# One DMA for the short set's rising rows, an earlier second gate chunk, Z cleared one step sooner, and newly searched units

## The chip, the cores and the metric

The kernel runs on one core of a Trainium2 chip. The metric is device time in microseconds (us) of one execution. The engines are TensorE (PE in the profile, its weight loads PEld), VectorE (DVE), ScalarE (ACT), GpSimd (POOL) and SyncE (SP, which here only issues DMAs). An engine's name with a q behind it (SPq) is its instruction queue.

## The reference

A two-dimensional Fourier transform of each of 8 sequences, its real part, and a SwiGLU block on the result.

```
x: [8, 3008, 256] f32;  w_gate, w_val: [256, 1536];  w_out: [1536, 256]
X = fft(fft(x, axis=1), axis=2).real          -> 24064 tokens of 256
g = X @ w_gate;   silu = g / (1 + exp(-g));   val = X @ w_val
out = (silu * val) @ w_out
```

## The kernel before

**What is computed where.** The real part of the transform is even under turning both frequencies, so the kernel computes for half of the tokens an even part (Pt) and an odd part (Qt). A token and its mirror are then made of the same two products, with Pt and Qt combined by plus and by minus. The transform along the 256 features is folded into the gate and value weights: Wp is the weights times a cosine table (CD), Wq the weights times a sine table (SDt), and Wm is Wq with the factor that the mirrored token needs. The transform along the 3008 rows is done by adding rows in pairs ("folding"), which shortens it, and then multiplying with cosine and sine tables (Tab).

**Prologue (lines 254 to 649).** It is written out by hand, engine by engine. Batch 0 is loaded in two sets: a long one into XA (128 partitions) and a short one into XC0. Rows that count upward ("rising") come in one way, rows that count downward ("falling") in another. For the short set, `rise_c` (line 263) is called twice, each time for one block of rising rows, and `fall_c` (line 266) four times for the falling ones. All of these go out from SyncE's queue. Permuting matmuls (`place`, line 431) put the rows in order, VectorE, GpSimd and ScalarE fold them (`cross`, `half_fold`, `fold_d`, `ends`, `heads`), and TensorE multiplies with Tab (`half_folded`, `folded_c`, `row0`), which gives Pt and Qt of the first tiles (`first_puts`). ScalarE fills the tables; `opposite(1)` (line 543) fills the last one, the negated columns for the short set, and the activation on line 544 clears Z0, a buffer of zeros. From Z0 two DMAs on SyncE (line 546) clear unused rows of XC, and behind them on the same queue go the first rows of batch 1 (`load_c`, lines 155 to 164).

The weights come in three chunks of 512 columns, gate and value apart, by DMAs that GpSimd issues (`load_w`, line 387). Chunk 0 goes into buffers of its own, chunks 1 and 2 into the part of XA that held the rising rows of batch 0. Each chunk is multiplied with CD and SDt on TensorE (`first_w`, line 500, for chunk 0; `weight_op`, line 1432, for the others, with the matmuls on line 1442). In GpSimd's order the loads of chunks 1 and 2 stand together, behind two folds `fold_d(1, 0)` and `fold_d(1, 2)` (line 495), the sum EOb (line 555) and the two `heads` adds for CEc (lines 462 and 463).

**Main part (lines 923 to 1667).** 24 tiles of mostly 512 half-set tokens, 12 units of 128 hidden columns in each: 288 units. A unit multiplies Pt and Qt with Wp, Wq and Wm (line 972) into PSUM tiles g and v, and ScalarE, VectorE and GpSimd make from them the two hidden products hp (the token) and hm (the mirrored one). The products of one tile are multiplied with w_out during the next tile (line 1236), copied out of PSUM (line 1243) and stored. In between stand the folds of later batches (GpSimd, lines 178 to 202), their transforms (line 1394) and the loads.

One digit per unit in `KINDS` says how it is done. The lowest bit: the value is "seeded", that is ScalarE writes a row into PSUM ahead of the matmuls (line 1045) and copies the even value out (line 1107), in place of one VectorE operation (line 1109). The second bit: the gate is split on VectorE, which saves one of the unit's five matmuls. From 4 on: ScalarE copies the value out and GpSimd makes hp (line 1192), from 8 on also the mirrored value (line 1195). A `w` unit does everything by whole matmuls.

The order of all this is made by a planner in the kernel itself (class `Sched`, line 767). Every operation gets a due time, that is the sum of TensorE's planned work so far plus a shift by kind (`SHIFT`) plus a correction by tile and kind (`BIAS_ROWS`). The planner then walks through planned time engine by engine and takes, within a window, what can start first. It uses planned durations, `W_AT` for the times at which the weight chunks of 1 and 2 land, and the start times of the engines that are given to `S.run` on the last line. What it decides is each engine's order of instructions, which the chip follows as it stands.

Of the kernel before, what the change touches and what calls it, by code (L numbers as in the profile page):

```python
# [15 lines left out]
AF = mybir.ActivationFunctionType  # L16
# [3 lines left out]
def kernel(  # L20
# [8 lines left out]
    nc = tc.nc  # L29
    B, M, D = x.shape  # L30
    Dff = moe_w_gate.shape[1]
    P = 128
# [3 lines left out]
    R = M // 4  # L36
# [53 lines left out]
    zero = const.tile([P, 1], F32, name="zero")  # L90
# [6 lines left out]
    Z0 = const.tile([P, 2, 3, P], BF16, name="Z0")  # L97
# [27 lines left out]
    def rows_at(b, row, ap):  # L125
        return bass.AP(tensor=x.tensor, offset=(b * M + row) * D, ap=ap)
# [124 lines left out]
    XC3 = XC0.rearrange("p a q d -> p a (q d)")  # L251
    q = nc.sync
# [7 lines left out]
    def fall_a(a, eng):  # L260
        eng.dma_start(out=XA3[:, 4 + a, :], in_=down_set(0, a, JA, LA, NA))

    def rise_c(a, eng):
        eng.dma_start(out=XC3[:, a, :], in_=rows_at(0, 2 * (P + 1) - 1 + a * R, [[2 * D, 64], [2 * R * D, 2], [1, 2 * D]]))

    def fall_c(hi, a, eng):
        eng.dma_start(out=XC3[64 * hi:64 * hi + NCR, 2 + a, :], in_=down_set(0, 3 - 2 * hi - a, JC, LC, NC_))
# [3 lines left out]
    fall_a(2, q)  # L271
    fall_a(1, nc.scalar)
    fall_a(0, q)
    for a in range(2):
        rise_c(a, q)

    iota = dict(channel_multiplier=0, allow_small_or_imprecise_dtypes=True)
    pcol = tp.tile([P, 1], F32, name="pcol")
# [102 lines left out]
    def opposite(ch):  # L381
        nc.scalar.activation(Tab[:, ch, :, :, NCE:NOO - 1], Tab[:, ch, :, :, GH + 1:NCE], AF.Copy, scale=-1.0)
# [1 line left out]
    def weigh_ce():  # L384
        nc.scalar.activation(Tab[:, 1, 1, :, 0:NCE], Tab[:, 1, 1, :, 0:NCE], AF.Copy, scale=wC)

    def load_w(c, only=(0, 1)):
        for i, src in ((0, moe_w_gate), (1, moe_w_val)):
            if i not in only:
                continue  # L390
            w_ = src.rearrange("(no p) f -> p no f", p=P)[:, :, c * T:(c + 1) * T]
            nc.gpsimd.dma_start(out=Wraw[i][:, :, (c - 1) * T:c * T] if c else W0[i], in_=w_)
# [10 lines left out]
                        in_=rows_at(0, 0, [[2 * R * D, 2], [R * D, 2], [1, D]]))  # L403
# [56 lines left out]
    def heads(ev, od, CE):  # L460

        ptt(CE[:, :, 0, 0, -1:], ev, od, op=Alu.add)
        ptt(CE[:, :, 0, 1, -1:], ev, od, op=Alu.subtract)
# [12 lines left out]
    def set_cols(ps, tab, a):  # L476
        if a % 2:
            return (ps[:, 0:2 * GH + 2].rearrange("p (t n) -> p t n", t=2),
                    tab[:, 0:2 * NCE].rearrange("p (t n) -> p t n", t=2)[:, :, 0:GH + 1])
        return ps[:, 0:NCE], tab[:, 0:NCE]  # L480

    def half_folded(eo, a0, first):
        for q in range(2):
            for a in range(a0, a0 + 2):
                dst, rhs = set_cols(acc[eo][q], Tab[:, 0, q, eo], a)
                nc.tensor.matmul(dst, EOb[:, eo, a, q, :], rhs, start=first and a == a0, stop=False, skip_group_check=True)

    def folded_c(eo, a, first=False):
        for q in range(2):
            dst, rhs = set_cols(acc[eo][q], Tab[:, 1, q, eo], a)  # L490
            nc.tensor.matmul(dst, EB[:, eo, a, q, :], rhs, start=first and a == 0, stop=a == 1, skip_group_check=True)

    def fold_d(eo, a0):
        F = FA[:, a0:a0 + 2]
        ptt(EOA[eo][a0 // 2], F[:, :, :, P:0:-1], F[:, :, :, P:D], op=SUMS[eo])

    def half_cast(eo, a0):
        nc.scalar.copy(EOb[:, eo, a0:a0 + 2], EOA[eo][a0 // 2])
# [24 lines left out]
    for a in range(2):  # L523
        ends(Eh[:, a], XA, psA, a)
    row_signs()
    load_w(0, (0,))
    fold_d(0, 0)
    load_w(0, (1,))
    fold_d(1, 0)
    for a in range(2, 4):  # L530
# [9 lines left out]
    for a in range(2, 4):  # L540
        nc.scalar.copy(FA[:, a, :, P + 1:D], psA[a][:, :, P + 1:D])
    half_cast(0, 2)
    opposite(1)
    nc.scalar.activation(Z0.rearrange("p q k d -> p (q k d)"), zero.to_broadcast([P, 6 * P]), AF.Copy)
    for hi in range(2):
        q.dma_start(out=X3c[64 * hi + NCR:64 * hi + 64, :].rearrange("p (c d) -> p c d", d=D),
                    in_=zeros[64 * hi + NCR:64 * hi + 64].unsqueeze(1).to_broadcast([64 - NCR, 16, D]))
    loads_c1 = load_c(1, q)
    for load in loads_c1[:C1_EARLY]:
        load()  # L550
    fold_d(1, 2)
    hd = tp.tile([P, 2, 2, 1], F32, name="hd")
    ptt(hd, Eh[:, 0:2], Eh[:, 2:4], op=Alu.add)
# [16 lines left out]
    for a in range(2):  # L570
        folded_c(1, a, True)
    half_folded(1, 0, False)
    heads(Ec0[:, 0], Ec0[:, 1], CEc)
    load_w(1)
    load_w(2)
    for k in range(2):
        pts(BBc[:, :, 1, k, 0:1], Ec0[:, 1 - k], scalar1=(nsgn, sgn)[k], scalar2=1.0, op0=Alu.mult, op1=Alu.mult)
    nc.gpsimd.iota(kfO, pattern=[[4, GH]], base=1, **iota)
# [104 lines left out]
    def rows(r0, n, step):  # L683
# [31 lines left out]
        "PUT": -2.8,  # L715
    }
    BIAS_ROWS = (
# [24 lines left out]
    )  # L742
    BIAS = {(t, k): v for t, row in enumerate(BIAS_ROWS) for k, v in zip(SHIFT, row)}
    ES_BUFS = 2
# [7 lines left out]
    GRP = 4  # L752
    AHEAD = 1
    WM_ACT = ()
    W_AT = (1.4, 2.8, 4.4, 6.0)
    SIGN_AT = 8
    class Op:
        __slots__ = ("eng", "dur", "lat", "fn", "at", "n", "deps", "owners", "new", "ring", "slots", "start", "end", "users")
# [161 lines left out]
    def pool_us(n):  # L920
# [6 lines left out]
    ROW_PE = {ROW_1: 1, ROW_2: 2, ROW_3: 3}  # L927
    KINDS = (
        "wwwwwwwwwwww",
        "06ww20001033",  # L930
        "031303160011",
        "010112310133",
        "010210112013",
        "10010b003133",
        "001211031052",
        "003171700001",
        "331213005030",
        "010271031100",
        "34130b310300",
        "01b300700101",  # L940
        "21312101b200",
        "001371310011",
        "70520031b212",
        "10310b030310",
        "001430103130",
        "413370000411",
        "213b21011200",
        "103b11309610",
        "0030b13300b0",
        "616444563010",  # L950
        "143034169230",
        "706120713313",
    )

    def whole(u):
# [18 lines left out]
    S = Sched()  # L974
# [631 lines left out]
    for fc in (1, 2):  # L1606
        for gv in range(2):
            S.add("DMA", 0.01, lambda: None, w=[(("W",), (fc, gv))], lat=W_AT[2 * fc - 2 + gv])
    S.add("DMA", 0.01, lambda: None, w=[(("pq", 0), "Q")], lat=0.1)
# [54 lines left out]
    part_b(prev)  # L1664
    owork = OWork(prev[0], ((psG, "g"), (psV, "v"), (psO, "o")))
    owork.run(len(owork.steps))
    S.run({'DVE': 1.5, 'ACT': 1.0, 'POOL': 1.6, 'PE': 0.0, 'SP': 1.0})


# [28 lines left out]
```

## Time and profile before

| | us |
|---|---|
| median of 3 runs | 603.52 |
| the 3 runs | 602.71, 603.52, 603.52 |
| the profiled execution's own time | 602.03 |
| its span, first to last instruction | 600.3 |
| TensorE busy in the span | 589.2 |
| first matmul of the main part's units | 19.07 |

How to read it: "busy" counts the time in which at least one instruction of the engine runs. Matmuls overlap, so their printed durations add up to more than their busy time; the distance from one start to the next is what a matmul costs. In a timeline a row has its start, its duration, engine, line, operation, tiles written and read, shapes, a count, and in brackets the idle time of the engine before it with what ended it. "DMA to landing" is the time from the start of the issue to the landing of the last byte.

### The profile page before, as it was taken

What the parts mean: (1) busy time and instruction counts of PE and PEld (TensorE: products, weight loads), DVE (VectorE), ACT (ScalarE), POOL (GpSimd) and SP (SyncE); (2) the same over time, 40 slices, a digit from 0 to 9 for tenths busy, and PEclk for the clock granted to TensorE, in tenths of its full rate; (3) what the DMA queues carried; (4) which work ended last, traced back from release to release, by engine and by line L of the source; (5) the groups of instructions that cost most, each with busy time, mean ns of one, the idle gap of its engine ahead of it and who ended that gap; (6) DMA issues with size and microseconds to landing.
All of it is one profiled execution on the core that took longest, in us unless ns stands there. A gap on an engine that the chain in (4) does not pass through costs nothing.

```text
span 600.3 us, 12453 instructions
## 1 busy us (share of the span) xinstructions
PE 589.2 (98%) x3950; PEld 390.3 (65%) x4012; DVE 568.3 (95%) x1063; ACT 556.4 (93%) x1081; POOL 529.1 (88%) x487
## 2 busy tenths in 40 slices
PE   9899999999999999999999999999999999999997
PEld 6356666666666666666666666666666666666686
DVE  8689999999999999999999999999999999999993
ACT  8587999999999999899999999998999999999994
POOL 8689999999799999999999999998898567687772
PEclk9899999999999999999999999999999999999999
DMA  9766347244625424444146122056221212111122
GB/s 243 117 125 131 108 124 183 77 131 117 157 81 123 126 69 120 112 142 127 55 96 144 45 55 72 19 119 157 62 63 37 64 31 70 55 44 45 50 62 80
DMA packets 51098, 57.65 MB, mean 96 GB/s; under 512 B 7299, under 2 KB 38455, under 8 KB 51033
## 3 DMA queue, kind: packets, MB, share of 16 engines
q1 hardware_dynamic: 47449, 53.91, 33.9%
q0 software_dynamic: 3216, 2.36, 2.8%
q8 instruction: 31, 0.51, 0.4%
q10 hardware_dynamic: 368, 0.59, 0.4%
q14 instruction: 34, 0.28, 0.2%
HBM read 29.43 MB, written 24.65 MB: 90 GB/s over the span
## 4 chain that ended last, share of the span: by engine, by line
PE 90%; ACT 3%; DMA 3%; POOL 2%; issue 1%; DVE 1%; SPq 0%; ACTq 0%; POOLq 0%
PE o L1236 38%; PE g L972 24%; PE v L972 20%; PE o L1394 2%; PE g L1394 2%; DMA XA<-in_moe_w_gate_dram 1%; DMA XA<-in_x_dram 1%; DMA out_dram<-ev 1%; PE o L304 1%; ACT sv L1159 1%; PE o L1442 1%; PE v L1236 1%; POOL hm L1183 1%; ACT v L1045 1%; ACT sp L1084 1%
## 5 line engine op out<-in xcount | busy, mean ns | idle before, releaser
L1183 POOL TENSOR_TENSOR hm<-sv 128x1024 bf16<-128x1024 f32 (+2 forms) x137 | 254.9, 1862 | 42.9 <-ACT sv L1159 25.1
L1175 DVE SCALAR_TENSOR_TENSOR sv<-es,v 128x512 f32<-128x512 f32 (+2 forms) x262 | 173.7, 669 | 4.8 <-PE v L972 3.5
L1236 PE MATMUL o<-Wo,hm 128*128 128x256 bf16 (+1 forms) x1128 | 164.2, 273 | 0.5
L1236 PE MATMUL o<-Wo,hp 128*128 128x256 bf16 (+1 forms) x1104 | 160.5, 273 | 0.6
L1186 DVE TENSOR_TENSOR hp<-sp,v 128x512 bf16<-128x512 f32 (+2 forms) x232 | 153.1, 669 | 2.2 <-ACT sp L1084 1.0
L1236 PEld LDWEIGHTS <-hm 128*128 128x128 bf16 (+2 forms) x1140 | 111.8, 98 | 57.6 <-issue 1.0
L1236 PEld LDWEIGHTS <-hp 128*128 128x128 bf16 (+2 forms) x1140 | 111.9, 98 | 56.3 <-issue 0.5
L1159 ACT ACTIVATE sv<-g 128x512 f32<-128x512 f32 (+2 forms) x179 | 119.0, 675 | 3.3 <-PE g L972 2.0
L1084 ACT ACTIVATE sp<-g 128x512 f32<-128x512 f32 (+2 forms) x179 | 110.4, 626 | 4.7 <-PE g L972 1.9
L1045 ACT ACTIVATE v<-bc,w 128x512 f32<-128x512 bf16 (+2 forms) x146 | 105.2, 721 | 1.2 <-DVE hp L1186 0.7
L972 PE MATMUL v<-Pt,Wp 128*128 128x512 bf16 (+2 forms) x285 | 105.0, 375 | 0.8
L972 PE MATMUL g<-Pt,Wp 128*128 128x512 bf16 (+2 forms) x282 | 105.5, 375 | 0.1
L1109 DVE SCALAR_TENSOR_TENSOR es<-bc,w,v 128x512 f32<-128x512 bf16 (+2 forms) x128 | 93.3, 733 | 2.5 <-POOL sv L1195 0.4
L1107 ACT ACTIVATE es<-v 128x512 f32<-128x512 f32 (+2 forms) x146 | 90.7, 623 | 3.8 <-DVE sv L1175 1.6
L972 PE MATMUL g<-Qt,Wq 128*128 128x512 bf16 (+2 forms) x247 | 90.9, 375 | 0.3
L972 PEld LDWEIGHTS <-Wp 128*128 128x128 bf16 x576 | 56.3, 98 | 27.3 <-issue 1.0
L972 PE MATMUL g<-Qt,Wm 128*128 128x512 bf16 (+2 forms) x188 | 70.8, 377 | 0.2
L1088 DVE SCALAR_TENSOR_TENSOR sg<-bc,w,g 128x512 f32<-128x512 bf16 (+2 forms) x95 | 68.6, 723 | 1.1 <-PE g L972 1.1
L1159 ACT ACTIVATE sv<-sg 128x512 f32<-128x512 f32 (+2 forms) x95 | 66.6, 705 | 1.7 <-DVE sg L1152 1.6
L1152 DVE SCALAR_TENSOR_TENSOR sg<-sg,g 128x512 f32<-128x512 f32 (+2 forms) x95 | 62.9, 662 | 0.4
L1156 ACT ACTIVATE sp<-g 128x512 f32<-128x512 f32 (+2 forms) x95 | 58.9, 620 | 2.1 <-DVE sg L1152 1.7
L1243 ACT COPY ev<-o 128x512 f32<-128x512 f32 x89 | 55.3, 621 | 4.3 <-PE o L1236 3.5
(218 smaller groups left out, 767.3 us busy)
## 6 DMA issues: line engine op xcount, KB each, us to landing
out_dram<-ev SPq DMA_DIRECT2D x96, 128.0 KB
XA<-in_x_dram SPq DMA_DIRECT2D x30, 256.0 KB
XA<-in_x_dram SPq DMA_DIRECT2D x112, 64.0 KB
XC<-in_x_dram SPq DMA_DIRECT2D x28, 120.0 KB
XC<-in_x_dram SPq DMA_DIRECT2D x105, 32.0 KB
bc<-br SPq DMA_DIRECT2D x19, 128.0 KB
St<-Fc SPq DMA_DIRECT2D x12, 128.5 KB
out_dram<-ev SPq DMA_DIRECT2D x12, 120.0 KB
```

The lines of the kernel that those rows point to most:

```text
L972: nc.tensor.matmul(ps[:, :n], Wt[:, gv, fs], src[:, :n], start=start, stop=stop, skip_group_check=True)
L1045: nc.scalar.activation(T_[kv][:, :w], bc[t][:, :w], AF.Copy, scale=w0[:, 1, f:f + 1])
L1084: nc.scalar.activation(sp_to()[:, :w], T_[kg][:, :w], AF.Silu)
L1088: nc.vector.scalar_tensor_tensor(T_[keg][:, :w], bc[t][:, :w], w0[:, 0, f:f + 1], T_[kg][:, :w], op0=Alu.mult, op1=Alu.add)
L1107: nc.scalar.activation(T_[kes][:, :w], T_[kv][:, :w], AF.Copy, scale=2.0 if on_pool(u) > 1 else 1.0)
L1109: nc.vector.scalar_tensor_tensor(T_[kes][:, :w], bc[t][:, :w], w0[:, 1, f:f + 1], T_[kv][:, :w], op0=Alu.mult, op1=Alu.add)
L1152: nc.vector.scalar_tensor_tensor(T_[kgm][:, :w], T_[keg][:, :w], 2.0, T_[kg][:, :w], op0=Alu.mult, op1=Alu.subtract)
L1159: nc.scalar.activation(sv()[:, f % 2, w - 1::-1, 1], T_[kgm if by_dve else kg][:, :w], AF.Silu)
L1175: nc.vector.scalar_tensor_tensor(sv()[:, f % 2, w - 1::-1, 0], T_[kes][:, :w], 2.0, T_[kv][:, :w], op0=Alu.mult, op1=Alu.subtract)
L1183: nc.gpsimd.tensor_tensor(hts_(t)[1][:, f - 1:f + 1, :w], sv()[:, :, :w, 1], sv()[:, :, :w, 0], op=Alu.mult)
L1186: nc.vector.tensor_tensor(hts_(t)[0][:, f, :wp], T_[ksp][:, :wp], T_[kv][:, :wp], op=Alu.mult)
L1236: nc.tensor.matmul(st["ps"][:n, j, :], hts[t][minus][:, f, c:c + n], Wo[:, f, :], start=(f == 0), stop=(f == nF - 1))
```

## The change

Four edits.

- The two rising-row DMAs of the short set become one with one more dimension (`rises_c`), with the same bytes to the same places.
- `load_w(1)` is split: the gate's chunk 1 is issued between `fold_d(1, 0)` and `fold_d(1, 2)` on GpSimd, the value's chunk 1 behind the EOb sum and ahead of the two `heads` adds for CEc. Chunk 2 stays behind these.
- Z0 is cleared ahead of `opposite(1)` on ScalarE instead of behind it.
- `BIAS_ROWS` (24 rows of 17 numbers), 16 rows of `KINDS`, `W_AT` and the start times for the planner are new numbers.

```diff
-    def rise_c(a, eng):
-        eng.dma_start(out=XC3[:, a, :], in_=rows_at(0, 2 * (P + 1) - 1 + a * R, [[2 * D, 64], [2 * R * D, 2], [1, 2 * D]]))
+    def rises_c(eng):
+        eng.dma_start(out=XC3[:, 0:2, :], in_=rows_at(0, 2 * (P + 1) - 1, [[2 * D, 64], [2 * R * D, 2], [R * D, 2], [1, 2 * D]]))
...
-    for a in range(2):
-        rise_c(a, q)
+    rises_c(q)
...
-    def load_w(c, only=(0, 1)):
+    def load_w(c, only):
...
     half_cast(0, 2)
+    nc.scalar.activation(Z0.rearrange("p q k d -> p (q k d)"), zero.to_broadcast([P, 6 * P]), AF.Copy)
     opposite(1)
-    nc.scalar.activation(Z0.rearrange("p q k d -> p (q k d)"), zero.to_broadcast([P, 6 * P]), AF.Copy)
...
         load()
+    load_w(1, (0,))
     fold_d(1, 2)
...
     half_folded(1, 0, False)
+    load_w(1, (1,))
     heads(Ec0[:, 0], Ec0[:, 1], CEc)
-    load_w(1)
-    load_w(2)
+    load_w(2, (0, 1))
...
-        (-13.7, -7.2, -11.75, -3.45, 3.2, -1.3, -1.15, 2.75, 7.55, -6.6, -9.45, -2, 3.85, -10.15, 18.65, -1.6, -4.05),
+        (-29.4, 13.3, 4.3, -0.95, -17.9, -7.05, 2.4, -8.1, -12.35, -6.85, -2.05, -18.8, -5.5, 1.6, -25.1, -6.8, -1),
...
-    W_AT = (1.4, 2.8, 4.4, 6.0)
+    W_AT = (0.0, 2.0, 3.2, 4.6)
...
-        "06ww20001033",
+        "06ww20001013",
...
-        "010112310133",
-        "010210112013",
-        "10010b003133",
-        "001211031052",
-        "003171700001",
+        "000010312133",
+        "010210112012",
+        "10110b103133",
+        "001601031052",
+        "300171700001",
...
-        "010271031100",
+        "010271031001",
...
-        "21312101b200",
+        "21312101b300",
...
-        "70520031b212",
-        "10310b030310",
-        "001430103130",
-        "413370000411",
+        "32120011b212",
+        "10130b135030",
+        "000135003170",
+        "033170001011",
...
-        "103b11309610",
-        "0030b13300b0",
-        "616444563010",
+        "103b10319610",
+        "4030b13300b0",
+        "616404563200",
...
-        "706120713313",
+        "706150233313",
...
-    S.run({'DVE': 1.5, 'ACT': 1.0, 'POOL': 1.6, 'PE': 0.0, 'SP': 1.0})
+    S.run({'DVE': 1.6, 'ACT': 1.0, 'POOL': 1.4, 'PE': 0.0, 'SP': 2.0})
```

46 rows, old and new, of the table BIAS_ROWS are left out of this document.

## The prediction

> **What bounds the kernel now.** I read the page first: the span, the busy time of each engine, and the chain of waits.
>
> ```profile
> span 600.3 us, 12453 instructions
> PE 589.2 (98%) x3950; PEld 390.3 (65%) x4012; DVE 568.3 (95%) x1063; ACT 556.4 (93%) x1081; POOL 529.1 (88%) x487
> PE 90%; ACT 3%; DMA 3%; POOL 2%; issue 1%; DVE 1%; SPq 0%; ACTq 0%; POOLq 0%
> ```
>
> TensorE (PE) is the bound: busy 98% of the span and 90% of the chain. So only two things can move the time: TensorE's idle or slowed stretches, and the number of its matmuls. Next came busy time by window. Columns: window; then us and count for PE, PEld, DVE, ACT, POOL; granted clock; DMA share; GB/s.
>
> ```profile
> 20.25:23.66 3.41, 1.18 (x7) 0.48 (x5) 1.31 (x4) 1.03 (x2) 3.36 (x8) 1.00 1.25 169
> 23.66:27.07 3.41, 3.41 (x10) 1.21 (x8) 1.13 (x2) 1.63 (x3) 1.43 (x2) 0.50 0.75 151
> 44.00:550.00 506.00, 502.92 (x3370) 333.68 (x3427) 494.37 (x884) 482.21 (x927) 464.20 (x396) 1.00 0.36 94
> 200.00:300.00 100.00, 99.37 (x668) 65.91 (x679) 98.76 (x180) 96.09 (x185) 98.17 (x85) 1.00 0.35 101
> ```
>
> From 44 to 550 TensorE is idle 3.1 us in 506, at full clock: there is almost nothing to win there, and much to lose, since the other three engines are 92 to 98% busy too. The one large hole is at 20 to 27 us: 3.41 us with 1.18 busy, then 3.41 us at half the clock. The timeline of TensorE says what is late there:
>
> ```profile
> 19.07 0.57 PE L972 MATMUL g<-Pt,Wp 128*128 128x480 bf16 x2
> 20.54 0.37 PE L972 MATMUL v<-Pt,Wp 128*128 128x480 bf16 x1
> 20.74 0.37 PE L972 MATMUL v<-Qt,Wq 128*128 128x480 bf16 x1
> 23.34 0.73 PE L1442 MATMUL o<-XA,CD 128*128 128x512 bf16 x2 [2.23 <-DMA XA<-in_moe_w_gate_dram]
> 27.50 0.59 PE L1442 MATMUL o<-XA,CD 128*128 128x512 bf16 x2
> 28.37 0.37 PE L972 MATMUL g<-Pt,Wp 128*128 128x480 bf16 x1
> 29.38 0.38 PE L1442 MATMUL o<-XA,CD 128*128 128x512 bf16 x1
> 31.66 0.59 PE L1442 MATMUL o<-XA,CD 128*128 128x512 bf16 x2
> ```
>
> The rows of L1442 are where the four remaining weight chunks are multiplied: gate 1 at 23.34, value 1 at 27.50, gate 2 at 29.38, value 2 at 31.66. Starts of L972 are 0.20 apart, so the first L1442 could have begun at 20.94: 2.40 us are lost to the gate's DMA. The half clock loses half of 3.41, 1.71 more. Together 4.1 us.
>
> **Part by part: the second gate chunk.** GpSimd's (POOL) timeline shows when the four chunks are issued. Behind it stands, for each of the four in that order, how long it took from issue to landing, and last the same for the value chunk before these, from the list of DMA issues.
>
> ```profile
> 11.33 1.11 POOL L495 TENSOR_TENSOR Fc<-FA 128x512 f32<-128x512 f32 x1
> 12.97 1.09 POOL L495 TENSOR_TENSOR Fc<-FA 128x512 f32<-128x512 f32 x1 [0.53 <-ACT FA L541]
> 14.61 1.27 POOL L555 TENSOR_TENSOR EOb<-Fc 128x512 bf16<-128x512 f32 x1
> 16.53 0.20 POOL L462 TENSOR_TENSOR CEc<-Ec 128x2 bf16<-128x2 f32 x1 [0.66 <-DVE Ec L453]
> 17.01 0.73 POOL L392 DMA_DIRECT2D XA<-in_moe_w_gate_dram  x1
> 17.74 0.74 POOL L392 DMA_DIRECT2D XA<-in_moe_w_val_dram  x1
> 18.46 0.73 POOL L392 DMA_DIRECT2D XA<-in_moe_w_gate_dram  x1
> 19.17 0.74 POOL L392 DMA_DIRECT2D XA<-in_moe_w_val_dram  x1
> ```
>
> ```profile
> DMA to landing us min/median/max: 6.3/6.3/6.3
> DMA to landing us min/median/max: 9.4/9.4/9.4
> DMA to landing us min/median/max: 10.1/10.1/10.1
> DMA to landing us min/median/max: 11.9/11.9/11.9
> ...
> W<-in_moe_w_val_dram POOLq DMA_DIRECT2D x1, 256.0 KB, 4.7
> ```
>
> Now they land at 23.3, 27.1, 28.6 and 31.1: each just ahead of its matmul, the first one after it. Gate 1 moves between the two folds, to about 12.45, four and a half us earlier. Its buffer's last readers, the placing matmuls, are done by 10, so it doesn't wait there. By 4.7 to 6.3 it lands at 17.1 to 18.8, well ahead of 20.94. That wait goes, and with it the half clock: -4.1.
>
> GpSimd pays 0.73 for the issue, of which 0.53 lies in an idle gap. Behind the issue on its queue stand the fold, three small adds and the EOb sum. L495's second fold starts at some 13.25, the EOb sum ends near 16.15 instead of 15.88. TensorE takes EOb at 16.71 (row below), so 0.5 us still cover it; without that cover it would cost the 0.3. Value 1 is then issued at 16.2, ahead of the two heads that waited until 16.53 anyway; they end near 17.3, and their readers start at 17.6.
>
> **What is late next.** Value 1 is now the first chunk under the load of SyncE's (SP) x rows, so I give it gate 1's 6.3: 22.5. TensorE wants it at 20.94 + 0.87 (four L1442, from 27.50 to 28.37) + 8 x 0.20 = 23.4. No wait, 0.9 to spare. Gate 2 is issued at 17.2; as second chunk, 9.4 gives 26.6, and the distance of first to second landing (27.1 - 23.3 = 3.8) gives 26.3. I take 26.4. The planner now takes it to land 3.2 after the first unit, at 19.07 + 3.2 = 22.3, and puts it after only three L972 instead of five: 23.4 + 0.87 + 0.61 = 24.9. So TensorE waits again, for 1.5 us. Value 2 comes 1.4 after gate 2 (28.6 - 27.1), at 27.8; it is wanted at 26.4 + 0.87 + 9 x 0.20 = 29.1 against 31.66 now. Net gain 2.6. The bounds: 0 new wait (4.1 gained), or the wait brings the half clock back (1.71 more, 0.9 gained).
>
> The row behind this is the 4.7 against 6.3 to 11.9 for equal chunks: those issued from 17 on are slower. The Trainium skill, DMA: Bandwidth & Descriptors, section on why a DMA increments its semaphore by 16, says that a transfer is spread over as many engines as divide its slowest dimension, and that the hardware queues take the lowest-numbered ones. By that, the zero fills and x rows of four partitions each all sit on the same four engines, where every chunk has a share, and gate 2 stays late: 600.9 by the sum below. Without it the 4.7 comes back and the time is 599.4. No view here names an engine.
>
> **The prologue edits.**
>
> ```profile
> 2.72 1.28 SPq L264 DMA_DIRECT2D XC<-in_x_dram  x2
> 4.04 6.47 SPq L267 DMA_DIRECT2D XC<-in_x_dram  x4
> 14.31 0.42 DVE L449 TENSOR_TENSOR FC<-o,XC 128x256 f32<-128x256 f32 x1 [0.39 <-DMA XC<-in_x_dram]
> 14.04 0.84 ACT L544 ACTIVATE Z<-zero 128x768 bf16<-128x768 f32 x1
> 14.90 1.49 SPq L546 DMA_DIRECT2D XC<-Z  x2
> 15.71 0.33 PE L491 MATMUL v<-Tab,EOf 128*128 128x378 bf16 x1 [0.25 <-DVE EOf L458]
> 16.71 0.48 PE L486 MATMUL v<-Tab,EOb 128*128 128x377 bf16 x2
> ```
>
> One DMA for both rising rows saves an issue of 0.64. More: in the built program SP's and ScalarE's DMAs take turns on eight completion flags, and one DMA less lets the last falling load wait for an earlier one (of 6.47 us for four issues of under 1.1 each, over 2 are waits). VectorE (DVE) waits 0.39 at 14.31 for it. That 0.39 may go; but the first place matmul for the short set now waits for both rises, and TensorE's queue, idle only 0.25 at 15.71, follows later. I book 0, from -0.4 to +0.3. Z moves ahead of the last table: the zero fills and all x rows behind them on SP start 0.84 sooner; the table ends near 15.0, and its reader on TensorE starts at 15.71, so 0.7 covers it, else up to 0.8 is lost.
>
> **The searched units.** Counted over all 24 rows, split gates stay 95, seeded values 146 and whole units 14, so TensorE's matmuls are the same number and cost 0. One product moves from GpSimd to VectorE. What is left is order: 0, from -1 (a third of the 3.1 idle) to +6 (below).
>
> Sum: 602.03 is the profiled execution's own time (span 600.3, 1.7 around it), the median 1.5 above. 602.0 - 4.1 + 1.5 = 599.4, on the median's scale 603.5 - 2.6 = **600.9**.
>
> **Rivals.**
> *No new wait* (0.20): SP's rows are drained when gate 2 comes; for it the 4.7, against it that all four chunks grew slower. 603.5 - 4.1 = 599.4.
> *The clock drops again* (0.13): idle 1.5 of a 3.41 window halves the next. For it: a window with 1.18 busy did so. Against it: this one would have 1.9 busy. 600.9 + 1.7 = 602.6, within 0.2%. The Trainium skill, TensorE: Matmul & The Clock Gate, section "Why this matters for your kernels", asks only that gaps stay under some 3 us; by it this rival is void and 600.9 stands. But the row shows half a clock after a gap of 2.2, so here the measurement decides and I keep it.
> *ScalarE (ACT) overflows* (0.17), slower. Rows 5, 12 and 15 of the units get 2, 1 and 1 more seeded values, row 15 one more value copied out. A seed and its copy are on ScalarE, in place of one VectorE operation:
>
> ```profile
> L1045 ACT ACTIVATE v<-bc,w 128x512 f32<-128x512 bf16 (+2 forms) x146 | 105.2, 721 | 1.2 <-DVE hp L1186 0.7
> L1107 ACT ACTIVATE es<-v 128x512 f32<-128x512 f32 (+2 forms) x146 | 90.7, 623 | 3.8 <-DVE sv L1175 1.6
> L1109 DVE SCALAR_TENSOR_TENSOR es<-bc,w,v 128x512 f32<-128x512 bf16 (+2 forms) x128 | 93.3, 733 | 2.5 <-POOL sv L1195 0.4
> ```
>
> 4 x (0.721 + 0.623) + 0.623 = 6.0 us more in three tiles of some 25 us, where ScalarE has about 1 us free each (96.09 of 100). If neither order nor neighbours absorb it, TensorE waits 3.0 to 6.0; it decides from 2.6 + 1.2 = 3.8 on. 600.9 + 4.5 = 605.4. Against it: rows 3, 4 and 6 lose as many.
> *It doesn't do what it says* (0.10): gate 1 lands late in spite of the early issue, behind x data still flowing at 12. 603.5.
>
> **How the numbers follow.** The forecast has 0.40, its own range 600.0 to 602.0. Faster means by over 0.2%, 1.2 us, about what a measurement of this kernel can tell from no change: below 602.3. Forecast, no new wait and the luckier third of the clock case: 0.64. Slower, above 604.7: 0.17. The rest, 0.19, within. The range leaves out the best of the second case and most of the fourth: 599.0 to 604.6.
>
> **What would show it.** In the profile after: gate 1's L392 between the two folds L494; no wait at the first L1442, which starts near 20.9; a wait of 1 to 2 us at the third (gate 2) at 25 to 26.5; granted clock 1.00 throughout 20 to 30; the 44 to 550 window as full as now. The prediction is wrong if the first L1442 still waits, if TensorE idles over 5 us in 44 to 550, or if the clock drops anywhere behind 7 us.

## The result, and the profile after

| | before | after |
|---|---|---|
| median, same chip (us) | 603.19 (602.71 to 603.52, 4 runs) | 599.10 (598.24 to 600.40, 4 runs) |
| the profiled execution's own time | 602.03 | 600.40 |
| its span | 600.3 | 598.6 |

The ratio of the times is 0.9935, with a 95% interval of 0.9913 to 0.9956: faster by 4.1 us. The two profiled executions are 1.6 us apart only. The one of before is below all four of its runs in the table, the one of after is the slowest of its four; why that matters comes with the explanation.

The page of the kernel after, its first lines and its chain of waits:

```profile
span 598.6 us, 12468 instructions
PE 587.0 (98%) x3953; PEld 389.2 (65%) x4012; DVE 570.3 (95%) x1064; ACT 557.4 (93%) x1080; POOL 527.8 (88%) x486
PE 71%; ACT 8%; DMA 6%; DVE 4%; POOL 3%; issue 3%; SPq 1%; ACTq 0%; POOLq 0%; DVEq 0%
```

TensorE's busy share is 98% as before, but its share of the chain fell from 90% to 71% (71% and 70% in the two later profiles of this kernel). So for some stretches something else sets the pace now; one of them is shown below.

Busy time of the kernel after in the two windows where before had its hole and its half clock:

```profile
20.25:23.66 3.41, 3.41 (x19) 1.60 (x17) 3.06 (x7) 2.39 (x6) 2.78 (x7) 1.00 0.96 166
23.66:27.07 3.41, 3.34 (x16) 1.44 (x16) 3.41 (x7) 2.71 (x6) 2.66 (x5) 1.00 0.80 123
```

The first is full (1.18 before), the second runs at clock 1.00 (0.50 before). The timeline of TensorE after, the matmuls of the four weight chunks and the one ahead of the third:

```profile
20.92 0.59 PE L1442 MATMUL o<-XA,CD 128*128 128x512 bf16 x2
...
23.40 0.59 PE L1442 MATMUL o<-XA,CD 128*128 128x512 bf16 x2
...
24.67 0.37 PE L972 MATMUL g<-Qt,Wm 128*128 128x480 bf16 x1
25.05 0.39 PE L1442 MATMUL o<-XA,CD 128*128 128x512 bf16 x1
...
27.75 0.59 PE L1442 MATMUL o<-XA,CD 128*128 128x512 bf16 x2
```

None has a wait in brackets. Only the third comes late: 0.38 behind the L972 ahead of it in place of 0.20, so 0.18. Value 2 is multiplied at 27.75, against 31.66 before: 3.91 us ahead. GpSimd's timeline after, and behind it the time from issue to landing of gate 1 and value 1, and of gate 2 and value 2 together (their least is gate 2's, their largest value 2's):

```profile
11.18 1.10 POOL L494 TENSOR_TENSOR Fc<-FA 128x512 f32<-128x512 f32 x1
12.21 0.73 POOL L391 DMA_DIRECT2D XA<-in_moe_w_gate_dram  x1
12.96 1.10 POOL L494 TENSOR_TENSOR Fc<-FA 128x512 f32<-128x512 f32 x1
...
14.60 1.27 POOL L555 TENSOR_TENSOR EOb<-Fc 128x512 bf16<-128x512 f32 x1
15.81 0.73 POOL L391 DMA_DIRECT2D XA<-in_moe_w_val_dram  x1
...
16.85 0.72 POOL L391 DMA_DIRECT2D XA<-in_moe_w_gate_dram  x1
17.57 0.73 POOL L391 DMA_DIRECT2D XA<-in_moe_w_val_dram  x1
```

```profile
DMA to landing us min/median/max: 4.4/4.4/4.4
DMA to landing us min/median/max: 7.4/7.4/7.4
DMA to landing us min/median/max: 8.2/9.0/9.8
```

Gate 1 lands at 12.21 + 4.4 = 16.6, value 1 at 23.2, gate 2 at 25.05, value 2 at 27.4.

**Where 2.7 us went again.** The last twelve matmuls start at these times, in TensorE's timeline of before and of after:

```profile
594.97 1.50 PE L1236 MATMUL g<-Wo,hm 128*64 128x256 bf16 x12
```

```profile
593.78 1.50 PE L1236 MATMUL g<-Wo,hm 128*64 128x256 bf16 x12
```

Of the lead of 3.91 at value 2, 1.19 is left at the end: 2.72 are given back between. The tail behind (600.3 - 594.97 = 5.33 against 598.6 - 593.78 = 4.82) returns 0.5; that is chance, since the copy control of before (e3_before_copy, below) has 4.8 too. Two of TensorE's three waits over 0.3 us between 45 and 112 in the kernel after (the third is 0.36 at 107.25, for ScalarE), and the chain of waits of after from 37 on:

```profile
64.74 0.38 PE L972 MATMUL g<-Pt,Wp 128*128 128x512 bf16 x1 [0.70 <-ACT sv L1159]
80.86 0.38 PE L972 MATMUL v<-Pt,Wp 128*128 128x512 bf16 x1 [0.55 <-DVE hp L1186]
```

```profile
37.71 0.42 PE g L972 x2
...
38.70 0.30 SPq L140
39.05 5.22 DMA XA<-in_x_dram
44.29 8.10 DMA XA<-in_x_dram
52.45 6.81 DMA XA<-in_x_dram
...
62.17 0.93 POOL hm L1183
...
83.01 0.65 ACT sv L1159
83.71 0.59 PE g L972 x2
```

The three waits make up 1.6 of the 2.72. The other 1.1 isn't waiting: from value 2 to the last matmuls TensorE's busy time is 561.2 against 560.1, and in before's second profile (below) it is 561.1 as well, so this part isn't shown to come from the change.

Read the chain downward: what ends last goes through TensorE until 38, then through SyncE's loads of batch 1's long set (L140) and their landings until 59.3, then through GpSimd's folds and the hm products that stand between them, and only at 83.7 back to TensorE. That stretch is 46 us, 8% of the span; what else lowers the share from 90% to 71% isn't shown here. It looks as if TensorE, four us earlier now, had caught up with batch 1's rows; the experiments put that to the test.

### The profile page after: what moved, and what is told of

Read it like the earlier page. It is cut to its first block, busy times and chain, and to the rows that moved or that the text cites. A ratio compares the mean times of both kernels' runs of the same rounds, so it can differ in the third digit from the quotient of the medians.

```text
span 598.6 us, 12468 instructions
## 1 busy us (share of the span) xinstructions
PE 587.0 (98%) x3953; PEld 389.2 (65%) x4012; DVE 570.3 (95%) x1064; ACT 557.4 (93%) x1080; POOL 527.8 (88%) x486
## 4 chain that ended last, share of the span: by engine, by line
PE 71%; ACT 8%; DMA 6%; DVE 4%; POOL 3%; issue 3%; SPq 1%; ACTq 0%; POOLq 0%; DVEq 0%
PE o L1236 30%; PE g L972 19%; PE v L972 16%; DMA XA<-in_x_dram 5%; ACT sv L1159 2%; PE o L1394 2%; PE g L1394 2%; ACT v L1045 2%; ACT es L1107 1%; POOL hm L1183 1%; DVE sv L1175 1%; ACT sp L1084 1%; DVE hp L1186 1%; ACT sp L1156 1%; ACT ev L1243 1%
## 5 line engine op out<-in xcount | busy, mean ns | idle before, releaser
L1159 ACT ACTIVATE sv<-g 128x512 f32<-128x512 f32 (+2 forms) x179 | 116.7, 671 | 4.6 <-PE g L972 2.3
L972 PE MATMUL v<-Pt,Wp 128*128 128x512 bf16 (+2 forms) x288 | 105.4, 375 | 1.8 <-DVE hp L1186 0.5
L972 PE MATMUL g<-Pt,Wp 128*128 128x512 bf16 (+2 forms) x280 | 104.4, 374 | 0.9 <-ACT sv L1159 0.7
L972 PE MATMUL g<-Qt,Wq 128*128 128x512 bf16 (+2 forms) x247 | 90.5, 374 | 0.4
L972 PEld LDWEIGHTS <-Wp 128*128 128x128 bf16 x576 | 56.3, 98 | 27.8 <-DVE Wp L505 0.7
L972 PE MATMUL g<-Qt,Wm 128*128 128x512 bf16 (+2 forms) x186 | 69.8, 375 | 0.2
L1159 ACT ACTIVATE sv<-sg 128x512 f32<-128x512 f32 (+2 forms) x95 | 65.1, 692 | 0.2 <-DVE sg L1152 0.2
L972 PE MATMUL v<-Qt,Wm 128*128 128x512 bf16 (+2 forms) x159 | 59.4, 374 | 0.8 <-ACT es L1107 0.4
```

Of the source, the lines that this page charges most:

```text
L972: nc.tensor.matmul(ps[:, :n], Wt[:, gv, fs], src[:, :n], start=start, stop=stop, skip_group_check=True)
L1159: nc.scalar.activation(sv()[:, f % 2, w - 1::-1, 1], T_[kgm if by_dve else kg][:, :w], AF.Silu)
```

## The experiments

"Before" is always the kernel before, run on the same chip beside the others; the ratio is to it.

**Both kernels again, and the change in two halves.** The prologue's edits alone (with before's numbers for the units), and the searched numbers alone (with before's prologue):

```diff
# e1_prologue: the change without these parts; e1_search: only these parts
     BIAS_ROWS = ( ... )
     KINDS = ( ... )
     W_AT = ( ... )
     S.run({ ... })
```

> The kernel before, once more, for a second profile. Both theories: a first wait of 2.2 to 2.4 us at the first L1442 for the gate chunk and half a clock for 3.41 us behind it; time 602.5 to 603.6. The profile of before had its own time (602.03) below the other runs: if these lose 0.7 to 1.5 us more in the main part, this profile shows where.

> The changed kernel, once more. The profile of after lost some 2.3 us in waits between 60 and 110 us and was the slowest of four runs (600.4 against 598.2 at best). If these waits come and go from run to run, this profile has fewer or other ones and a time of 598.2 to 599.6; if they belong to the order, they stand at the same places again.

> All prologue edits, the unit numbers of before. Theory P (the gain is the gate's wait, 2.40, and the half clock, 1.71): no wait at the first L1442, clock 1.00 throughout, 599 to 600.5. Theory S (the new unit numbers are needed to keep the gain, because the old order was made for later chunks): the wait goes, but 1.5 us or more come back between 28 and 120 us, 601 or more.

> The new unit numbers alone, the prologue of before. Theory P: the first L1442 still waits 2.2 to 2.4 and the clock halves; the third chunk, which the new order wants earlier, may wait too; 603 to 606. Theory S: 601 to 602.5, faster than before.

Measured, beside 604.70 for before: before again 603.12, ratio 0.9991 (0.9971 to 1.0011), which is the size of the noise; after again 599.47, 0.9923 (0.9901 to 0.9945); the prologue alone 601.02, 0.9937 (0.9914 to 0.9960); the search alone 604.23, 0.9984 (0.9963 to 1.0005). The prologue carries the gain. The search alone can't be told from nothing, as theory P had it; nor can what it adds to the prologue, as these two intervals overlap.

After's waits belong to its order: in the repeat they stand at the same places, smaller, with 0.29 at 64.56 and 0.55 at 80.69 (0.18 and 0.55 in e3_after, below). From value 2 to the last matmuls it is 566.03 in the first profile, 565.25 and 565.05 in these two. Of the five profiles of kernels that still have the stall, four take 563.3 to 563.7 and before's second one takes 565.04. So the give-back is 2.72 only in the pair of profiles above, and one profile can be off by 1.7.

The prologue alone, with before's own order of the units, gives back as much, 566.68, and TensorE, which waits nowhere between 36 and 112 in before, has a larger wait there:

```profile
76.93 0.85 PE L972 MATMUL g<-Pt,Wp 128*128 128x512 bf16 x2 [1.48 <-ACT sv L1159]
```

So theory S was right that 1.5 us or more come back (and 601.02 is in its range, not in P's 599 to 600.5, though before was 1.2 slower here than in the prediction) but not in its reason: the old order loses them and the new one does too.

In before's second profile the wait that the change removes was over twice as long. TensorE's timeline of that run, and two stretches of 3.41 us of it:

```profile
26.00 1.01 PE L1442 MATMUL o<-XA,CD 128*128 128x512 bf16 x2 [5.13 <-DMA XA<-in_moe_w_gate_dram]
```

```profile
22.01:25.42 3.41, 0.00 (x0) 0.00 (x0) 0.08 (x1) 0.00 (x0) 1.36 (x4) 1.00 1.09 194
25.42:28.83 3.41, 2.83 (x7) 0.99 (x7) 0.69 (x1) 0.93 (x2) 0.25 (x1) 0.50 0.37 86
```

The wait is 5.13 in place of 2.23, and the half clock follows as in the first profile.

**The prologue in two.** The split of the weight loads alone, and the other two edits alone:

```diff
# e2_gate: kernel before, and only
+    load_w(1, (0,))
     fold_d(1, 2)
...
+    load_w(1, (1,))
     heads(Ec0[:, 0], Ec0[:, 1], CEc)
-    load_w(1)
# e2_rises_z: kernel before, with rises_c and Z0 cleared ahead of opposite(1), and load_w(1) where it was
```

> The kernel before, with only the split of the weight loads (gate chunk 1 between the two folds, value chunk 1 ahead of the two heads); rises, Z and units as before. Theory G: the issue of the gate's chunk is all that removes the wait and the half clock, so this gives what the whole prologue gave (ratio 0.994 to 0.996, 600.5 to 602): no wait at the first L1442, full clock from 20 to 30 us, gate 2 late by 0 to 1.5 us. Rival H: half of the gain is the x rows of batch 1, which the one DMA and the earlier Z start 1 us sooner and so clear the way for gate 2: then this gives 0.997 to 0.998 (602 to 602.5) and gate 2 is waited for, 2 us or more.

> The kernel before, with only the one DMA for the rising rows and Z ahead of the last table. Theory G: 0.999 to 1.001 (603 to 604), the wait at the first L1442 stays above 2 us and the half clock behind it stays. Rival H: 0.997 to 0.998. Both expect the zero fills about 1 us sooner than before's 14.90 and VectorE's wait of 0.39 at 14.31 gone.

Measured, beside 604.31: the split 601.99, 0.9961 (0.9947 to 0.9976); the other two edits 603.90, 0.9989 (0.9975 to 1.0003). The split gives most of it; it came out below the whole prologue, but the intervals overlap. TensorE's timelines, first with the split alone (where that line is 1443), then with the other two edits alone (line 1441):

```profile
24.76 0.61 PE L1443 MATMUL o<-XA,CD 128*128 128x512 bf16 x2 [0.99 <-DMA XA<-in_moe_w_val_dram]
```

```profile
25.15 1.01 PE L1441 MATMUL o<-XA,CD 128*128 128x512 bf16 x2 [3.82 <-DMA XA<-in_moe_w_gate_dram]
```

With the split alone gate 1 comes in time (its matmul starts at 21.12 without a wait), and value 1 is waited for by 0.99. In this run, with the x rows not moved up, the second chunk is late; in the kernel after the same chunk landed 0.2 us ahead of its matmul. That the rows' place is the reason isn't shown: a later run with the whole prologue (e4_copy_act, below) waits 0.75 for it too. With the other two edits alone the zero fills go out at 14.16 in place of 14.90, as expected, and the wait for gate 1 stays. So the rising rows and Z can't be told from nothing by themselves, and what they add to the split isn't settled. Both ratios are nearest to theory G; their intervals still reach H's 0.997 to 0.998.

**Are batch 1's rows what gives the time back?** First they were made later. The copy within XC, the last load of batch 1's short set, was issued twice; and, with another aim, the falling loads of the long set were given to ScalarE's queue:

```diff
# e2_copy_twice: kernel after, and
-        c=[lambda: q.dma_start(out=XC[0:NCR, 0:4, 1], in_=XC[r, 0:4, 0])])
+        c=[lambda: [q.dma_start(out=XC[0:NCR, 0:4, 1], in_=XC[r, 0:4, 0]) for _ in range(2)]])
# e2_downs_act: kernel after, and in load_a
-                [lambda a=a: q.dma_start(out=X3[:, 4 + a, :], ...) for a in range(4)])
+                [lambda a=a: (nc.scalar if b == 1 else q).dma_start(out=X3[:, 4 + a, :], ...) for a in range(4)])
```

> The changed kernel, with SyncE's copy within XC (the last load of batch 1's short set, line 169) issued twice; everything else and its order the same. It puts one more 240 KB transfer between the loads of the short and the long set of batch 1. Theory L (the changed kernel's new waits of 1.4 to 2.2 us between 60 and 110 us come from batch 1's rows landing too late for GpSimd's folds): the fold of the long set (line 178, 59.5 to 59.7) starts 1 to 2.5 us later and TensorE waits that much more between 60 and 110, so 600.3 to 601.5. Rival O (they come from the order of the units alone, with GpSimd's folds not deciding): the fold is later too, but the time stays within 0.5 us of the changed kernel's.

> The changed kernel, with the four falling loads of batch 1's long set (line 142) issued by ScalarE's queue in place of SyncE's, at the same places of the order; nothing else differs. ScalarE has 1.5 to 2 us free in each 5 us between 40 and 50 and pays some 0.6 us for each issue. Theory L: the fold of the long set starts 1 to 2 us sooner than 59.5, the waits at 64, 80 and 83 us shrink to under 0.5 in all, and the time falls by 0.8 to 1.5 us, to 597.8 to 598.5. Rival O: the fold is sooner, the waits stay, and the time is the same or up to 1 us more (ScalarE pays). If the bytes and not the issue set the pace, the fold does not come sooner at all.

Measured, beside 604.31: 603.74, 0.9992 (0.9975 to 1.0008), and 619.85, 1.0257 (1.0242 to 1.0272), against 0.9923 to 0.9935 for the kernel after in its three sets of runs. The first is slower than either theory said. The second is a miss: it was to bring the rows sooner. GpSimd's timeline of the first fold of batch 1's short set, in the kernel after, with the copy doubled, and with the loads on ScalarE's queue, and from this last SyncE's timeline:

```profile
42.33 2.36 POOL L178 TENSOR_TENSOR SDf<-XC 128x1020 f32<-128x1020 f32 x1 [2.06 <-DMA XA<-in_x_dram]
```

```profile
46.19 2.36 POOL L178 TENSOR_TENSOR SDf<-XC 128x1020 f32<-128x1020 f32 x1 [5.26 <-DMA XA<-in_x_dram]
```

```profile
62.49 2.34 POOL L178 TENSOR_TENSOR SDf<-XC 128x1020 f32<-128x1020 f32 x1 [21.51 <-DMA XC<-XC]
```

```profile
29.23 14.08 SPq L155 DMA_DIRECT2D XC<-in_x_dram  x2
```

The releaser in the first two rows is a transfer of XA, which this fold doesn't read: it is only the one that came last by the profile. SyncE stood 14 us at two loads of the short set, until 43.31; ScalarE had issued the first of the long set's loads at 39.69. What SyncE waited for at that line, by its list of waits (total, times, longest):

```profile
SPq L155 <- DMA XA<-in_x_dram: 21.8, 8, 13.3
```

The semaphore records of this trace say what that is: the DMAs of SyncE and ScalarE use eight completion flags in turn, and each waits for the last use of its own. The load that SyncE issued at 43.06 has the flag of ScalarE's load of 39.69 and waited for that one. For the folds, what counts is the dose: folds later by 3.86 and 20.16, the time higher than 599.47 by 4.3 and 20.4. How it reaches TensorE is seen with the copy doubled, in the timelines of ScalarE and TensorE:

```profile
58.90 0.60 ACT L1084 ACTIVATE sp<-g 128x512 f32<-128x512 f32 x1 [2.92 <-POOL hp L1192]
59.39 0.69 ACT L1045 ACTIVATE v<-bc,w 128x512 f32<-128x512 bf16 x1
```

```profile
60.13 0.38 PE L972 MATMUL v<-Pt,Wp 128*128 128x512 bf16 x1 [2.83 <-ACT v L1045]
```

The product hp stands behind the fold in GpSimd's order; ScalarE waits 2.92 for it, and TensorE 2.83 for the seed that ScalarE writes next. So 3.86 of lateness made 2.83 of waiting; the rest of the 4.3 is the clock, which ran at half for some 3.4 us (1.7 lost). The window just behind the wait holds most of that:

```profile
60.10:63.50 3.40, 3.37 (x15) 1.88 (x15) 1.29 (x2) 2.37 (x5) 0.66 (x2) 0.66 0.50 128
```

The next expectation's words that a late fold costs its whole lateness are right in their sum only: some 1 us of it is covered, and a halved clock makes up for that.

**Then they were made sooner.** One ScalarE instruction makes the copy within XC in place of the DMA, in the kernel after and, as a control, in the kernel before:

```diff
-        c=[lambda: q.dma_start(out=XC[0:NCR, 0:4, 1], in_=XC[r, 0:4, 0])])
+        c=[lambda: nc.scalar.copy(XC[0:NCR, 0:4, 1], XC[r, 0:4, 0])])
```

> The changed kernel again, as the one beside which the next is read: 598.5 to 600, ratio 0.992 to 0.9935, some 1.4 to 2.2 us of waits of TensorE between 60 and 110 us, the fold of batch 1's short set starting at 42.3 to 42.6.

> The changed kernel, with the copy within XC (line 169, partitions 64 on to 0 on, 240 KB) made by one ScalarE instruction in place of SyncE's DMA; nothing else moves in any engine's order. Two earlier runs delayed that fold by 3.9 and 20.2 us and the time rose by 4.4 and 20.5, so a late fold costs its whole lateness; this one takes lateness away. The DMA takes some 5 us from its issue at 36.8 to the fold's start at 42.3; ScalarE's copy should take 1 to 1.5 us in a place where it has 1.07 us idle, so the fold starts at 40.3 to 41 (GpSimd is free at 40.27) and SyncE's loads of the long set come 0.9 sooner. Theory L: the waits between 60 and 110 shrink below 1 us and the time falls 0.7 to 1.5 us below the changed kernel's of the same call. Rival O (order of the units): folds sooner, waits the same, time within 0.4 us. A third way: ScalarE's later work there is pushed by 1 us and TensorE waits for it: 0.5 to 1 us slower.

> The kernel before, with the same edit (ScalarE makes the copy within XC). There GpSimd waits only 0.8 us for batch 1's rows and TensorE hardly waits between 60 and 110 us, as its half clock and its wait for the gate's chunk have put it 4 us behind. Theory L: no gain, 0.9985 to 1.0005. If it gains 1 us or more, as in the changed kernel, then the copy costs something else than what L says.

> The kernel of e3_copy_act again, since its interval there overlaps the changed kernel's. Theory L: TensorE's waits between 60 and 110 us stay under 0.5 us in all, and the ratio stands at 0.990 to 0.992, below the 0.9923, 0.9926 and 0.9935 of the changed kernel. If it comes out at 0.9925 or above, the waits it takes away are paid back in a place that the trace does not name.

Measured, beside 604.75: after again 600.21, 0.9926 (0.9911 to 0.9941); with the copy on ScalarE 599.58, 0.9915 (0.9898 to 0.9931); before with that copy 604.05, 0.9986 (0.9968 to 1.0004). In the last set, on another chip, the copy on ScalarE stood beside before alone (603.09): 599.85, 0.9941 (0.9922 to 0.9960). ScalarE's timeline, GpSimd's first folds of the short and the long set, and TensorE's value 2 and last matmuls, all of e3_copy_act:

```profile
36.30 1.04 ACT L169 COPY XC<-XC 60x1024 f32<-60x1024 f32 x1 [0.57 <-DMA XC<-in_x_dram]
```

```profile
39.93 2.35 POOL L178 TENSOR_TENSOR SDf<-XC 128x1020 f32<-128x1020 f32 x1
...
57.35 2.36 POOL L178 TENSOR_TENSOR SDf<-XA 128x1020 f32<-128x1020 f32 x1
```

```profile
27.44 0.59 PE L1442 MATMUL o<-XA,CD 128*128 128x512 bf16 x2
...
591.56 1.50 PE L1236 MATMUL g<-Wo,hm 128*64 128x256 bf16 x12
```

The copy takes 1.04 and both folds start 2.3 to 2.4 us sooner, without waiting. From value 2 to the last matmuls it is 564.12, against 566.03, 565.25 and 565.05 in the three profiles of the kernel after: 1.91 of the 2.72 are back by the first pair, 0.9 by the last. The repeat agrees in this, from 28.91 to 593.08, that is 564.17. TensorE's share of the chain is 79% in the first run; in the page of e4_copy_act it is TensorE's own chain again:

```profile
PE 92%; POOL 3%; DMA 2%; DVE 1%; issue 1%; SPq 0%; ACT 0%; POOLq 0%; ACTq 0%
```

But in the repeat TensorE was late already at value 2, by waits for two chunks that lie ahead of the edit:

```profile
24.24 0.61 PE L1442 MATMUL o<-XA,CD 128*128 128x512 bf16 x2 [0.75 <-DMA XA<-in_moe_w_val_dram]
...
26.22 0.60 PE L1442 MATMUL o<-XA,CD 128*128 128x512 bf16 x2 [0.33 <-DMA XA<-in_moe_w_gate_dram]
```

And the times don't show the gain: 0.63 us in the set that had both, with intervals that overlap, and 0.9941 in the one without the kernel after beside it. The repeat's expectation called that a payment in a place that the trace does not name; the trace does name 1.1 us of it, in these two rows, ahead of the edit. So the folds are shown to be what the waits from 60 on hang on: sooner folds take them away, with TensorE's list of waits empty behind value 2 in both runs, and later folds make them larger. Which fold, the short set's or the long set's, wasn't tried apart, since the edit moves both. The chain of after names the long set's; with the copy doubled it was the short set's, as the wait of 2.83 ended at 60.13 and the long set's fold began at 63.46. Whether the copy on ScalarE beats the changed kernel is not settled. In before it gains nothing that can be told from the noise, as theory L had it: there the cover is still in place.

## Why the prediction held, and where its steps did not

- **The bound and the two places** held. The first L1442 was put at 20.94 and came at 20.92, without a wait; the clock stayed at 1.00. Gate 1 was to be issued at 12.45 and land by 17.1 to 18.8: 12.21 and 16.6.
- **What hides the issue** held, and more. The EOb sum was to end 0.3 late; it starts at 14.60 (14.61 before). The two folds start at 11.18 and 12.96 (11.33 and 12.97): the issue took up the idle 0.53 and what the first fold had gained.
- **The new wait for gate 2 was mis-sized**: 1.5 by the sum, 0.18 measured. Its matmul was wanted at 24.87 (24.9 by the sum), but the chunk was issued at 16.85 in place of 17.2 and took 8.2 in place of the 9.4 taken from before. That is 1.3 of the 1.5 us by which the gain came out larger than forecast (4.1 against 2.6); the time came below the forecast's own range of 600.0 to 602.0. In the two later profiles of after this matmul doesn't wait at all. The rival "no new wait" had the outcome at this place, 599.4, for another reason than its own: the landing didn't fall back to 4.7. Value 1, given 0.9 to spare, had 0.2, and in the run with the split alone it was late by 0.99: the sum saw the danger at gate 2 only, and at value 1 it is as large.
- **The clock rival** wasn't put to the test by a 0.18 wait, but its size of gap came elsewhere. The run with the split alone had a gap of 0.99, and behind it the clock stayed at 1.00 (23.4 to 27.0 with 2.61 of 3.60 busy). The prologue alone had 1.48 at 76.93: its window from 74.17 to 77.58 had 1.83 of 3.41 busy, where the prediction reckoned with 1.9, and the clock stayed at 1.00 too. Every gap of 2.2 and more behind 20 us in these profiles was followed by half the clock. The search alone, two windows in a row:

```profile
19.58:22.99 3.41, 1.19 (x5) 0.50 (x6) 1.70 (x5) 1.03 (x2) 3.40 (x10) 1.00 1.29 159
22.99:26.40 3.41, 3.24 (x8) 1.13 (x8) 2.05 (x6) 1.06 (x2) 0.99 (x2) 0.50 0.92 177
```

  The wait there was 2.34. So the clock held with 1.83 busy and dropped with 1.19: the rival would most likely have failed with the forecast wait too. The Trainium skill, TensorE: Matmul & The Clock Gate, section "Why this matters for your kernels", asks only for gaps under some 3 us. These runs differ from it, since gaps of 2.23, 2.34 and 2.83 were followed by half the clock.
- **The prologue's other edits at 0** held for the two alone (0.9989). As booked, VectorE's wait of 0.39 went and the first place matmul took one over, in TensorE's timeline of after:

```profile
11.27 1.95 PE L435 MATMUL o<-XC,putC 128*128 128x512 f32 x4 [0.99 <-DMA XC<-in_x_dram]
```

  Yet L490, in the place of L491, comes at 15.53 against 15.71.
- **The units at 0** held within what can be measured (0.9984 alone; 0.9937 to 0.9923 on top of the prologue). ScalarE didn't overflow: behind 112 us TensorE's list of waits is empty in after. The count behind that rival left out row 17, which gets one more seeded value as well, and row 21, which loses one.
- **The window from 44 to 550, "as full as now", was wrong**, though it stayed under the 5 us of idle time that would have refuted the whole: TensorE is idle for 4.7 us in it, against 3.1 (4.0 and 3.8 in the later profiles). 2.72 us are given back from value 2 on in the first pair of profiles, of which 1.6 are waits; all of the waits go with sooner folds. The step "what is late next" asked this only of the four weight chunks, not of batch 1's rows on SyncE's queue, whose folds had 4 us of cover from the very stall that was to go. The rows moved up by less than TensorE did: the short set's first fold from 44.09 to 42.33, the long set's from 60.60 to 59.65.

```profile
44.09 2.35 POOL L178 TENSOR_TENSOR SDf<-XC 128x1020 f32<-128x1020 f32 x1 [0.77 <-DMA XA<-in_x_dram]
...
60.60 2.36 POOL L178 TENSOR_TENSOR SDf<-XA 128x1020 f32<-128x1020 f32 x1 [0.28 <-DMA XC<-in_x_dram]
```

  These are before's; after's are 42.33, above, and 59.65 at the end of the chain's last landing.
- **Two errors offset each other, so the closeness of the sum is in part luck.** On the scale of the profiled executions the sum gives 602.03 - 2.6 = 599.4, and 600.40 came: 1.0 slower, since the give-back is larger than the mis-sized wait. On the scale of the medians it was 1.8 faster, since the profiled run of before was a lucky one: its wait was 2.23, the second profile of before had 5.13, and the three experiments that left the weight loads in place had 2.34, 3.82 and 4.53. So 4.1 is near the least that before loses at this stall, and adding the same 1.5 to the sum with and without it took a part of the stall for a constant.

## What to carry to other kernels

A stall early in a kernel is cover for every transfer behind it. Before pricing its removal, list what lands during or after it, and ask of each how much sooner it comes itself; what doesn't move is the next bound. A wait for a DMA has a spread: take it from several runs, as one profile may show the best case. And when an experiment moves a DMA to another queue, look at what the first queue then waits for.

## What the hardware showed that was not expected

The wait for the same chunk under the same loads differed between runs by 2.9 us (2.23 and 5.13 in two profiles of the kernel before); from value 2 to the last matmuls the same two differ by 1.7, and three of the kernel after by 1.0. The clock held after a window of 3.41 us with 1.83 busy and halved after one with 1.19. A copy of 240 KB from partitions 64 on to partitions 0 on took ScalarE 1.04 us, while with the DMA the fold that needs it started 5.5 us after its issue at 36.80. And four loads moved to a second queue stopped the first one for 14 us, through a completion flag that both use.
